# Two interleaved transformer layers on one core: an unsplit copy of half 0's last bank, interleaved scores in half 1, memory scores between weightings, and up weights loaded in the value part

## The chip, the cores and the metric

The kernel runs on one core of a Trainium2 chip. The metric is device time in microseconds; three executions of the kernel before took 1604.5, 1606.29 and 1607.28 us, so the median is 1606.29 us.

Five engines matter: TensorE (PE in the profile, and PEld for its weight loads, which overlap the matmuls), VectorE (DVE), ScalarE (ACT), GpSimd (POOL) and SyncE (SP), which issues most of the DMAs. TensorE writes its results into PSUM, which the kernel uses as eight banks; ACT and DVE copy them out to on-chip memory.

## The reference, cut to what matters

```
x = x + A(layernorm(x));  x = x + B(layernorm(x))     # done twice, with the same weights

A: for each of 64 segments of 32 tokens:
     h = concat(mem, segment)                # 8 memory rows + 32 token rows = 40 rows of 448
     q, k, v = h Wq, h Wk, h Wv              # 16 heads of 256
     p = softmax(mask(q k^T / 16))
     o = (p v) Wo
     mem = o[first 8 rows]                   # goes into the next segment
     output rows = o[other 32 rows]
B: (relu(x W_gate) * (x W_up)) W_down        # 448 -> 1792 -> 448
```

The memory makes attention a chain over segments: segment s+1 can't start before segment s has given its memory.

## The kernel before, in words

**Folded weights.** Per head, Wq and Wk are multiplied once into a 448x448 matrix (`A_sb`), and Wv and Wo into another (`B_sb`). This is the setup, in the pool `pre`: a loop over eight pairs of heads builds `A_sb` (the query-key part, lines 358-393) and a second one builds `B_sb` (the value part, lines 395-418). The raw weights are turned over by `flips` (line 307) into tiles with the tag `tT`, six buffers. The Wo blocks come by `load_wo` (line 349) over POOL's queue into four buffers with the tag `wo`; four are asked for in the last four passes of the query-key part, and each pass p of the value part asks for block p+4 at its end. `spread` (line 87) makes such a DMA wait for the TensorE instruction that was last in the program.

**Steps.** After the setup, 69 calls of `step` (line 680) follow. Step g works on segment g of the first layer pass ("chain 0") and on segment g-4 of the second ("chain 1"), so their 2 x 40 = 80 rows are the columns of one matmul. Steps 0 to 3 and 64 to 67 have one chain only, 40 columns. Heads are split in two halves (hf = 0, 1) of eight.

In a step, `project` (line 594) multiplies the rows with `A_sb`. A half is 28 tiles of 128, in five PSUM banks: tiles 0-5, 6-11, 12-17, 18-23 and 24-27; the copies go to `TQ` (the four banks of six tiles) and `TZ` (the bank of four). `BANKS` (line 42) sets the order; bank 18 comes last in both halves. `project_early` (line 581) does the 64-row part of four banks ahead. Then come the scores: `scores_m(hf)` (line 710) for the memory rows, into a bank `Sm`, and `scores_x(hf)` (line 718) for the token rows, into a bank `Sx`. Each score sums over four blocks kd of the 448 features in the order `KD = (0, 1, 3, 2)`: kd 0 and 1 read banks 0, 6 and 12, kd 3 reads `TZ`, and kd 2 reads banks 12 and 18. `softmax` (line 642) gives three pieces of work that the step places itself: maximum and difference on DVE, the exponential on ACT, the sum and the division on DVE. `flipped` turns the probabilities over on TensorE (tile `pps`, copied to `PT`), `weigh_m` (line 730) and `weigh_x` (line 743) multiply them with the rows (`ya`, `yb`; `y1`, `y2`) and copy the result to `Y`, and `project_out` and `project_last` multiply `Y` with `B_sb` into `ox` and `o`. The weighting of half 1's token rows is put off into the next step, as `late` (line 848), between `project_early(1, ...)` and half 1's projection.

**The feed-forward layer.** Every second step of the middle carries a `Feed` (here "a feed step"; the others are "plain steps"): 128 rows are normalised (`xn`), turned over (`tps`, `xT`), multiplied with W_up and W_gate (`ups`, `gps`), gated (`hh`, on DVE) and multiplied with W_down (`dps`). `open_rows` (line 488) takes four banks at a time and does the 64-row part first. W_up, W_gate and W_down are loaded in 28 pieces, one per call of `next_piece` (line 455), from step 0 on: 7 for W_up, 7 for W_gate, 14 for W_down.

**What sets the order.** All matmuls are chained in the order of the program (`in_order`, line 79), and after the setup DVE's and ACT's instructions are too (`InOrder`, line 92). A PSUM bank is chosen by `bank` (line 120): of the banks not held, the one that an own clock in the program says comes free first. A new tile in a bank waits for the last reader of the old one.

**The split copy.** In feed steps, half 0's bank 18 leaves PSUM in two copies on ACT (`quick`, lines 600, 620 and 631): tiles 0-2 after their nine matmuls, tiles 3-5 after the bank's last. Both halves lie in the same bank, and the matmuls of tiles 3-5 come behind the first copy.

Of the kernel before, what the change touches and what calls it, by code (L numbers as in the profile page):

```python
# [8 lines left out]
BF = mybir.dt.bfloat16  # L9
F32 = mybir.dt.float32  # L10
# [5 lines left out]
DM = 448  # L16
H = 16
NP = 8
# [3 lines left out]
L = MEM + SEG  # L22
F = 1792
# [36 lines left out]
def build_kernel(ctx, tc, A_x, A_mem0, A_Wq, A_Wk, A_Wv, A_Wo, B_W_gate, B_W_up, B_W_down, out,  # L60
# [149 lines left out]
    A_sb = glob.tile([P, 4, 2, NT, 128], BF, name="A_sb")  # L210
    B_sb = glob.tile([P, 2, NT, DM], BF, name="B_sb")

    hTb = []
    for i in range(2):
        t = glob.tile([P, BLK, HW], BF, name=f"hT{i}")
# [57 lines left out]
    with tc.tile_pool(name="pre", bufs=6) as pre:  # L273
# [32 lines left out]

        def flips(src, p, name):
            nat = load_nat(src, p, nc.sync)
            o = pre.tile([P, 4, 512], BF, tag="tT", name=name)

            def half(e2):
                tp = bank([P, 2, 512], BF, "tpw")
                n = 3 if src is Wv else 4
                for kd in range(n):
                    for e in range(2):
                        tr(tp[:, e, kd * 128:(kd + 1) * 128],
                           nat[:, kd, (2 * e2 + e) * 128:(2 * e2 + e + 1) * 128], ident[:])
# [29 lines left out]
        wos = []  # L347

        def load_wo(p):
            wos.append(pre.tile([P, 4, DM], BF, tag="wo", name="wo", bufs=4))  # L350
            spread(nc.gpsimd.dma_start(wos[-1][:], Wo[:, 4 * p:4 * p + 4, :]))

        ready, todo = queue(0)
# [4 lines left out]
        for p in range(NP):  # L358
# [26 lines left out]
                        todo.pop(0)()  # L385
            share(A_sb[:, 0:3, hf, 24 + p4, :], mx_ps[:, 0:3, :], 384, (1.28, 0.85))
            share(A_sb[0:64, 3, hf, 24 + p4, :], mx_ps[0:64, 3, :], 128, (1.28, 0.85))
            if p >= 4:
                load_wo(p - 4)
            if p == 1:  # L390
                xn0 = normed(row_stats(xp[1]))
            if p == 2:
# [2 lines left out]
        for p in range(NP):  # L395
            hf, p4 = divmod(p, 4)
            vT = ready
            ready, todo = flips(Wv, p + 1, "vT") if p + 1 < NP else (None, [])
            wo = wos.pop(0)
            for eo in range(2):  # L400
                for kd in range(3):
                    bps = bank([P, 512], F32, "bps")
                    for t in range(2):
                        e = 2 * eo + t
                        mm(bps[:, 0:DM], vT[:, e, kd * 128:(kd + 1) * 128], wo[:, e, :],
                           start=(t == 0), stop=(t == 1))
                    share(B_sb[:, hf, tidx(kd, eo, p4), 0:DM], bps[:, 0:DM], DM, (1.28, 0.85))
                    if kd == 1 and todo:
                        todo.pop(0)()
            bps = bank([P, 512], F32, "bps")  # L410
            for t in range(2):
                for eo in range(2):
                    e = 2 * eo + t
                    mm(bps[64 * eo:64 * eo + 64, 0:DM], v3[:, p, e, :], wo[:, e, :],
                       start=(t == 0), stop=(t == 1), tile_position=(0, 64 * eo))
            share(B_sb[:, hf, 24 + p4, 0:DM], bps[:, 0:DM], DM, (1.28, 0.85))
            if p + 4 < NP:
                load_wo(p + 4)

    for i in range(min(3, nblk)):  # L420
        nc.gpsimd.memset(xa[i][:], 0.0)
# [19 lines left out]
    nc.gpsimd.memset(hh[:], 0.0)  # L441

    Wg_sb = main.tile([P, 4, F], BF, name="Wg_sb")
    Wu_sb = main.tile([P, 4, F], BF, name="Wu_sb")
    Wd_sb = main.tile([P, FT, DM], BF, name="Wd_sb")
    pieces = []
    for dst, src in ((Wu_sb, B_W_up), (Wg_sb, B_W_gate)):
        for k in range(3):
            for cols in (slice(0, F // 2), slice(F // 2, F)):
                pieces.append((dst[:, k, cols], src[128 * k:128 * k + 128, cols]))  # L450
        pieces.append((dst[FR[src is B_W_gate], 3, :], src[384:448]))
    for f in range(FT):
        pieces.append((Wd_sb[:, f, :], B_W_down[128 * f:128 * f + 128]))

    def next_piece():

        if pieces:
            spread(nc.sync.dma_start(*pieces.pop(0)))


    class Feed:

# [131 lines left out]
    def project(hf, chains, hb, j, banks, pre={}, busy=False, first=None, inside=None):  # L594

        n = L * len(chains)
        for i0, k in banks:
            ps = pre[i0] if i0 in pre else bank([P, 512], F32, "prj")
            two = len(chains) == 2
            quick = busy and not hf and i0 == 18  # L600

            def copies(eng, rows, T, a, b):
                T = T.rearrange("p g (t q) -> p t g q", q=16)
                if two:
                    evac(eng, T, ps[rows, a * n:b * n].rearrange("p (t g q) -> p t g q", t=b - a, q=16))
                    return
                c = chains[0]
                src = ps[rows, a * n:b * n].rearrange("p (t w) -> p t w", t=b - a)
# [5 lines left out]
            def tq(a, b):  # L614
                return TQ[hf][:].rearrange("p g u w -> p g (u w)")[:, :, 16 * (i0 + a):16 * (i0 + b)]
# [12 lines left out]
            if first is not None:  # L628
                first()
            if i0 < 24:  # L630
                a = 3 if quick else 0
                copies(act if (i0 != 6 if busy and hf else i0 % 12) else dve, slice(0, P), tq(a, k), a, k)
            else:
                copies(act if busy else dve, slice(0, 64), TZ[hf][0:64, :, 0:64], 0, k)
                copies(act, slice(64, 128), TZ[hf][64:128, :, 64:128], 0, k)
            if i0 in (6, 18):
                next_piece()

# [41 lines left out]
    def step(g, ff, pre, late):  # L680
# [26 lines left out]
            act.copy(hk[:, 4, 64:128], kps[:, 3, 64:128])  # L707
            return hk

        def scores_m(hf):  # L710
            if not ms:
                return (lambda: None,) * 3
            Sp = bank([P, 2, L], F32, "Sm", 1100)
            for kd in KD:
                mm(Sp[:, :, :], queries(hf, 2, kd), moving(hb, j, kd, (0, 1)), start=(kd == KD[0]), stop=(kd == KD[-1]))
            return softmax(Sp, 2, PM[hf], blk[:], f"m{hf}")

        def scores_x(hf):
            Sp = bank([P, 4, L], F32, "Sx", 2500 if hf == 0 else 3500 if ff is None else 8000)
            both = len(chains) == 2  # L720
            if not both:
                mm(Sp[:, :, :], ident[:], maskS[:], start=True, stop=False, skip_group_check=True)
            for half in range(2):
                for c in chains:
                    for kd in KD:
                        mm(Sp[:, 2 * half + c, :], queries(hf, 3 * c + half, kd), moving(hb, j, kd, (c,)),
                           start=(both and kd == KD[0]), stop=(kd == KD[-1]), skip_group_check=True)
            return softmax(Sp, 4, PX[hf], None, f"x{hf}", maskS[:] if len(chains) == 2 else None)

        def weigh_m(hf, hk, PT):  # L730
            if not ms:
# [11 lines left out]
        def weigh_x(hf, hk, PT):  # L743

            def keep(eng, c, t0, src):
                n = src.shape[-1] // SEG
# [98 lines left out]
        if ff is not None:  # L845
            ff.norm()
        pre1 = project_early(1, chains, hb, j)
        if late is not None:
            late()
        if len(chains) == 1:  # L850
            m0 = scores_m(0)
            m0[0]()
            m0[1]()
        project(1, chains, hb, j, BANKS[1][0:1], pre1, True)
        if len(chains) == 2:
            m0 = scores_m(0)
            m0[0]()
            m0[1]()
# [11 lines left out]
        project(1, chains, hb, j, BANKS[1][4:5], pre1, True, None, flip_m0)  # L870
        if ff is not None:
            ff.xposed_out()
        x0 = scores_x(0)
        weigh_m(0, hk, pm)
        m1 = scores_m(1)
        m1[0]()
        m1[1]()
        x1 = scores_x(1)
        x0[0]()
        if end:  # L880
            ff.open_rows((0, 1))
# [42 lines left out]
        else:  # L924
# [118 lines left out]
```

## Time and profile before

| what | value |
|---|---|
| median of three runs | 1606.29 us |
| the profiled execution | 1606.33 us |
| its span, first to last instruction | 1604.4 us |
| PE busy / PEld busy | 1573.1 us (98%) / 1445.3 us (90%) |
| DVE / ACT / POOL busy | 1133.0 (71%) / 757.4 (47%) / 77.4 us (5%) |
| granted TensorE clock | 1.00 |
| DMA, mean over the span | 21 GB/s; 200 to 330 GB/s in the first 50 us |
| share of PE in the chain that ended last | 96% |

The profiled execution lies 0.04 us from the median, and 1.9 us of it are outside the span. Two things are needed to read the profile. A matmul's end is modelled: an 80-column matmul is shown with 202 ns, though the next one starts some 36 ns after it. So a stall is seen better between the starts of two matmuls than in idle time, which is smaller by the part of the 202 ns that lies over it. And a group of matmuls in the timeline ends about 0.2 us after the start of its last one.

By time, the span has: the query-key part until about 48 us, the value part until about 75 us, one-chain steps with the loads of the feed-forward weights until about 145 us, pairs of a plain and a feed step with two chains from there to about 1516 us (30 such feed steps, one every 45.9 us), and the one-chain steps and the last feed at the end.

### The profile page before, as it was taken

The page shows a single profiled execution, that of the slowest core. Times are in us where ns is not written, and L with a number is a line of the kernel's source. Part 1 is how long each engine was busy: PE and PEld are TensorE (multiplying, and loading weights), DVE is VectorE, ACT ScalarE, POOL GpSimd, SP SyncE. Part 2 cuts the span into 40 slices and gives each one's busy share as a digit, 9 for nine tenths or more (in the row PEclk, how much of TensorE's full clock was granted, in tenths as well). Part 3 has the DMA queues.
Part 4 walks back from the last instruction along what each step waited for, and adds up shares of the span by engine and source line. Part 5 has one row for each costly group of instructions (what it writes and reads, how often), then busy time and mean ns, then how long its engine had stood idle before and what let it go on. Part 6 is the DMA issues. An engine that isn't in the chain of part 4 may idle for free.

```text
span 1604.4 us, 89783 instructions
## 1 busy us (share of the span) xinstructions
PE 1573.1 (98%) x41132; PEld 1445.3 (90%) x41132; DVE 1133.0 (71%) x3706; ACT 757.4 (47%) x2126; POOL 77.4 (5%) x172
## 2 busy tenths in 40 slices
PE   9999999999999999999999999999999999999998
PEld 6688999999999999999999999999999999999897
DVE  8766777777677777776777777767777777667765
ACT  5644444454444444544444445444444454444443
POOL 3200000000000000000000000000000000000000
PEclk9999999999999999999999999999999999999999
DMA  8530000000000000000000000000000000000000
GB/s 242 163 107 15 8 9 9 10 4 9 9 10 9 9 9 9 4 9 10 9 9 9 9 8 5 10 9 9 9 9 9 7 5 10 9 8 6 7 7 6
DMA packets 27755, 33.12 MB, mean 21 GB/s; under 512 B 3560, under 2 KB 26480, under 8 KB 27376
## 3 DMA queue, kind: packets, MB, share of 16 engines
q1 hardware_dynamic: 26288, 23.70, 5.3%
q8 instruction: 321, 5.26, 1.3%
q0 software_dynamic: 1088, 3.68, 0.8%
q14 instruction: 58, 0.48, 0.1%
HBM read 23.70 MB, written 1.84 MB: 16 GB/s over the span
## 4 chain that ended last, share of the span: by engine, by line
PE 96%; ACT 1%; DVE 1%; issue 1%; DMA 0%; SPq 0%; POOLq 0%; ACTq 0%; POOL 0%
PE prj L143 31%; PE ox L143 25%; PE ups L143 7%; PE dps L143 5%; PE gps L143 5%; PE o L143 5%; PE y L143 4%; PE Sx L143 3%; PE pps L151 2%; PE Sm L143 2%; PE bps L143 1%; PE aps L143 1%; PE tpw L151 1%; PE ya L143 1%; PE tps L151 1%; PE yb L143 1%
## 5 line engine op out<-in xcount | busy, mean ns | idle before, releaser
L143 PE MATMUL prj<-hT,A_sb 128*128 128x80 bf16 (+3 forms) x15232 | 547.1, 199 | 17.3 <-ACT TQ L101 16.6
L143 PEld LDWEIGHTS <-A_sb 128*128 128x128 bf16 (+1 forms) x15232 | 500.8, 99 | 42.9 <-issue 21.2
L143 PEld LDWEIGHTS <-B_sb 128*128 128x128 bf16 (+1 forms) x15232 | 490.6, 103 | 14.5 <-issue 1.0
L143 PE MATMUL ox<-Y,B_sb 128*128 128x80 bf16 (+3 forms) x11424 | 440.3, 199 | 0.9 <-issue 0.9
L101 ACT CAST TQ<-prj 128x480 bf16<-128x480 f32 (+5 forms) x416 | 189.6, 466 | 111.4 <-PE prj L143 101.4
L101 DVE CAST Y<-y 128x256 bf16<-128x256 f32 x376 | 151.4, 457 | 55.5 <-PE y L143 55.4
L101 ACT CAST Y<-y 128x512 bf16<-128x512 f32 (+2 forms) x392 | 136.6, 419 | 103.4 <-PE y L143 103.2
L101 ACT ACTIVATE se<-se 128x80 f32<-128x80 f32 (+1 forms) x270 | 81.9, 303 | 165.5 <-DVE se L101 161.2
L143 PE MATMUL gps<-xT,Wg_sb 128*128 128x128 bf16 (+3 forms) x1904 | 133.9, 216 | 0.0
L101 DVE CAST TQ<-prj 128x480 bf16<-128x480 f32 (+1 forms) x228 | 128.4, 572 | 7.5 <-PE prj L143 7.0
L143 PE MATMUL ups<-xT,Wu_sb 128*128 128x128 bf16 (+3 forms) x1904 | 132.3, 216 | 0.5 <-DVE xT L101 0.5
L101 DVE SCALAR_TENSOR_TENSOR hh<-gps,ut 128x512 bf16<-128x512 f32 (+2 forms) x136 | 80.2, 592 | 47.6 <-PE ya L143 41.4
L143 PEld LDWEIGHTS <-Wu_sb 128*128 128x128 bf16 (+1 forms) x1904 | 105.0, 97 | 8.0
L143 PEld LDWEIGHTS <-hk 40*128 40x128 bf16 (+1 forms) x1950 | 99.4, 96 | 10.7 <-issue 2.5
L143 PEld LDWEIGHTS <-Wg_sb 128*128 128x128 bf16 (+1 forms) x1904 | 106.9, 97 | 0.5 <-issue 0.5
L101 ACT CAST TZ<-prj 64x320 bf16<-64x320 f32 (+2 forms) x264 | 96.8, 377 | 17.2 <-DVE TZ L101 13.6
L101 ACT COPY os<-o 64x16 f32<-64x16 f32 (+3 forms) x135 | 25.8, 191 | 162.2 <-PE o L143 160.6
L101 DVE TENSOR_REDUCE ssum<-se 128x2 f32<-128x80 f32 (+1 forms) x270 | 73.7, 273 | 37.5 <-ACT se L101 37.5
L143 PE MATMUL dps<-Wd_sb,hh 128*128 128x448 bf16 (+1 forms) x476 | 93.1, 353 | 0.0
L143 PEld LDWEIGHTS <-TQ 128*128 128x128 bf16 x1938 | 87.1, 97 | 6.0 <-issue 0.4
L143 PE MATMUL y<-PT,hk 40*128 40x256 bf16 (+1 forms) x1280 | 86.7, 248 | 1.6 <-ACT PT L101 1.0
L235 POOL TENSOR_SCALAR rstd<-mv 128x1 f32<-128x1 f32 x67 | 14.8, 221 | 1467.2 <-DVE mv L101 1467.2
(118 smaller groups left out, 1920.0 us busy)
## 6 DMA issues: line engine op xcount, KB each, us to landing
wo<-in_A_Wo_dram POOLq DMA_DIRECT2D x8, 448.0 KB, 4.6
nat<-in_A_Wq_dram SPq DMA_DIRECT2D x8, 384.0 KB, 4.9
nat<-in_A_Wk_dram SPq DMA_DIRECT2D x8, 384.0 KB, 5.0
nat<-in_A_Wv_dram SPq DMA_DIRECT2D x8, 384.0 KB, 5.7
xa<-in_A_x_dram SPq DMA_DIRECT2D x32, 56.0 KB, 2.2
xa<-xp SPq DMA_DIRECT2D x32, 56.0 KB, 1.9
out_dram<-xa SPq DMA_DIRECT2D x32, 56.0 KB, 2.3
xp<-in_A_x_dram SPq DMA_DIRECT2D x30, 56.0 KB, 2.6
```

The costliest lines, as they stand in the source:

```text
L101: r = f(*a, **k)
L143: in_order(nc.tensor.matmul(out, lhsT, rhs, **k))
L151: in_order(nc.tensor.transpose(out, src, idn))
L235: nc.gpsimd.tensor_scalar(out=rstd[:], in0=mv[:, 1:2], scalar1=EPS, scalar2=None, op0=ALU.add)
```

## The change

Five edits:

1. `quick` is gone: bank 18 of half 0 leaves in one copy after its last matmul, in feed steps too.
2. `scores_m` and `scores_x` become one function `scores(hf, m, x)`. For half 1 it does the memory and the token scores together: first all matmuls of the blocks kd 0, 1 and 3 of both, then those of kd 2. Half 0 keeps its order.
3. W_up's tile is taken at the start of the kernel, outside the pools, and its seven pieces are asked for in the value part, two at the end of each pass from p = 3 on. To make room, `tT` has four buffers instead of six and `wo` three instead of four; Wo's first three blocks are asked for in the last three passes of the query-key part, and pass p of the value part asks for block p+3. The calls of `next_piece` in the steps stay, and begin with W_gate.
4. In one-chain steps half 0's memory scores, with the first two pieces of their softmax, move from behind the late weighting into it, between the copies of `y1` and the matmuls of `y2`.
5. In plain one-chain steps the turn of half 1's memory probabilities comes after 23 instead of 22 tiles of `project_out`.

```diff
+    Wu_sb = glob.tile([P, 4, F], BF, name="Wu_sb")
...
+    pieces = weights(Wu_sb, B_W_up)
...
-            o = pre.tile([P, 4, 512], BF, tag="tT", name=name)
+            o = pre.tile([P, 4, 512], BF, tag="tT", name=name, bufs=4)
...
-            wos.append(pre.tile([P, 4, DM], BF, tag="wo", name="wo", bufs=4))
+            wos.append(pre.tile([P, 4, DM], BF, tag="wo", name="wo", bufs=3))
...
-            if p >= 4:
-                load_wo(p - 4)
+            if p >= 5:
+                load_wo(p - 5)
...
-            if p + 4 < NP:
-                load_wo(p + 4)
+            if p + 3 < NP:
+                load_wo(p + 3)
+            if p >= 3:
+                next_piece()
+                next_piece()
...
+    pieces += weights(Wg_sb, B_W_gate)
...
-            quick = busy and not hf and i0 == 18
...
-                if quick and i == 3:
-                    copies(act, slice(0, P), tq(0, 3), 0, 3)
...
-        def scores_m(hf):
-        def scores_x(hf):
+        def scores(hf, m, x):
...
+            def mem(kds):
+                for kd in kds:
+                    mm(Sm[:, :, :], queries(hf, 2, kd), moving(hb, j, kd, (0, 1)),
+                       start=(kd == KD[0]), stop=(kd == KD[-1]), skip_group_check=True)
+
+            def own(kds):
+                for half, c in groups:
+                    for kd in kds:
+                        mm(Sx[:, 2 * half + c, :], queries(hf, 3 * c + half, kd), moving(hb, j, kd, (c,)),
+                           start=(both and kd == KD[0] and (half, c) == groups[0]), stop=(kd == KD[-1]),
+                           skip_group_check=True)
...
+            if m and x:
+                mem(KD[:3])
+                mask()
+                own(KD[:3])
+                mem(KD[3:])
+                own(KD[3:])
...
             for c in chains:
                 keep(act if c == 0 or len(chains) == 1 else dve, c, 0, y1[c][:])
+            if between is not None:
+                between()
             y2 = {c: bank([P, 384], F32, f"y2_{c}", 1300) for c in chains}
...
-            late()
-        if len(chains) == 1:
-            m0 = scores_m(0)
+            late(memory_0 if len(chains) == 1 else None)
+        if len(chains) == 1 and late is None:
+            memory_0()
...
-        x0 = scores_x(0)
+        _, x0 = scores(0, False, True)
         weigh_m(0, hk, pm)
-        m1 = scores_m(1)
+        m1, x1 = scores(1, True, True)
         m1[0]()
         m1[1]()
-        x1 = scores_x(1)
         x0[0]()
...
-            late_flip = 23 if hi - lo == W else 22
+            late_flip = 23
...
-        return pre, lambda: weigh_x(1, hk, px1)
+        return pre, lambda between: weigh_x(1, hk, px1, between)
```

`memory_0` is `scores(0, True, False)` and the first two pieces of its softmax; in two-chain steps it is called where `scores_m(0)` was.

More of the change, by code (lines that the diff above doesn't have):

```diff
@@ L211, in build_kernel, with weights, next_piece @@
     B_sb = glob.tile([P, 2, NT, DM], BF, name="B_sb")
+    Wu_sb = glob.tile([P, 4, F], BF, name="Wu_sb")
+    def weights(dst, src):
+        return [(dst[:, k, cols], src[128 * k:128 * k + 128, cols])
+                for k in range(3) for cols in (slice(0, F // 2), slice(F // 2, F))] + [
+                    (dst[FR[src is B_W_gate], 3, :], src[384:448])]
+    pieces = weights(Wu_sb, B_W_up)
+    def next_piece():
+        if pieces:
+            spread(nc.sync.dma_start(*pieces.pop(0)))
     hTb = []
@@ L443, in build_kernel @@
     Wg_sb = main.tile([P, 4, F], BF, name="Wg_sb")
-    Wu_sb = main.tile([P, 4, F], BF, name="Wu_sb")
+    pieces += weights(Wg_sb, B_W_gate)
     Wd_sb = main.tile([P, FT, DM], BF, name="Wd_sb")
[L446 to L451, printed above, removed]
     for f in range(FT):
         pieces.append((Wd_sb[:, f, :], B_W_down[128 * f:128 * f + 128]))
-    def next_piece():
-        if pieces:
-            spread(nc.sync.dma_start(*pieces.pop(0)))
     class Feed:
@@ L599, in project, with copies @@
             two = len(chains) == 2
-            quick = busy and not hf and i0 == 18
-            def copies(eng, rows, T, a, b):
+            def copies(eng, rows, T):
                 T = T.rearrange("p g (t q) -> p t g q", q=16)
                 if two:
-                    evac(eng, T, ps[rows, a * n:b * n].rearrange("p (t g q) -> p t g q", t=b - a, q=16))
+                    evac(eng, T, ps[rows, 0:k * n].rearrange("p (t g q) -> p t g q", t=k, q=16))
                     return
                 c = chains[0]
-                src = ps[rows, a * n:b * n].rearrange("p (t w) -> p t w", t=b - a)
+                src = ps[rows, 0:k * n].rearrange("p (t w) -> p t w", t=k)
                 x, m = (0, SEG) if c == 0 else (MEM, 0)
@@ L612, in copies @@
                      src[:, :, x:x + SEG].rearrange("p t (g q) -> p t g q", q=16))
-            def tq(a, b):
-                return TQ[hf][:].rearrange("p g u w -> p g (u w)")[:, :, 16 * (i0 + a):16 * (i0 + b)]
             for i in range(k):
@@ L630, in project @@
             if i0 < 24:
-                a = 3 if quick else 0
-                copies(act if (i0 != 6 if busy and hf else i0 % 12) else dve, slice(0, P), tq(a, k), a, k)
-            else:
-                copies(act if busy else dve, slice(0, 64), TZ[hf][0:64, :, 0:64], 0, k)
-                copies(act, slice(64, 128), TZ[hf][64:128, :, 64:128], 0, k)
+                T = TQ[hf][:].rearrange("p g u w -> p g (u w)")[:, :, 16 * i0:16 * (i0 + k)]
+                copies(act if (i0 != 6 if busy and hf else i0 % 12) else dve, slice(0, P), T)
+            else:
+                copies(act if busy else dve, slice(0, 64), TZ[hf][0:64, :, 0:64])
+                copies(act, slice(64, 128), TZ[hf][64:128, :, 64:128])
             if i0 in (6, 18):
@@ L708, in hk_make, with mask @@
             return hk
-        def scores_m(hf):
+        def scores(hf, m, x):
             if not ms:
[L712 to L716, printed above, removed]
-        def scores_x(hf):
-            Sp = bank([P, 4, L], F32, "Sx", 2500 if hf == 0 else 3500 if ff is None else 8000)
-            both = len(chains) == 2
[L721 to L728, printed above, removed]
+                m = False
+            both = len(chains) == 2
+            Sm = bank([P, 2, L], F32, "Sm", 1100) if m else None
+            Sx = bank([P, 4, L], F32, "Sx", 2500 if hf == 0 else 3500 if ff is None else 8000) if x else None
+            groups = [(half, c) for half in range(2) for c in chains]
+            def mem(kds):
[8 more added lines that the diff above has]
+                           skip_group_check=True)
+            def mask():
+                if not both:
+                    mm(Sx[:, :, :], ident[:], maskS[:], start=True, stop=False, skip_group_check=True)
+            if m and x:
[4 more added lines that the diff above has]
+                own(KD[3:])
+            elif m:
+                mem(KD)
+            elif x:
+                mask()
+                own(KD)
+            sm = softmax(Sm, 2, PM[hf], blk[:], f"m{hf}") if m else (lambda: None,) * 3
+            sx = softmax(Sx, 4, PX[hf], None, f"x{hf}", maskS[:] if both else None) if x else None
+            return sm, sx
@@ L741, in weigh_m, with weigh_x @@
             act.copy(YB[hf][:, 16:28, M0:M0 + 16], yb[:].rearrange("p (t q) -> p t q", q=16))
-        def weigh_x(hf, hk, PT):
+        def weigh_x(hf, hk, PT, between=None):
             def keep(eng, c, t0, src):
@@ L847, in step, with memory_0 @@
         pre1 = project_early(1, chains, hb, j)
-        if late is not None:
-            late()
-        if len(chains) == 1:
-            m0 = scores_m(0)
+        m0 = None
+        def memory_0():
+            nonlocal m0
+            m0, _ = scores(0, True, False)
             m0[0]()
             m0[1]()
+        if late is not None:
+            late(memory_0 if len(chains) == 1 else None)
+        if len(chains) == 1 and late is None:
+            memory_0()
         project(1, chains, hb, j, BANKS[1][0:1], pre1, True)
         if len(chains) == 2:
-            m0 = scores_m(0)
-            m0[0]()
-            m0[1]()
+            memory_0()
         project(1, chains, hb, j, BANKS[1][1:2], pre1, True, m0[2])
```

## The prediction

> **What bounds the kernel now.** I read the page's busy shares first, then who waited for whom, then the timeline of one feed step, matmul by matmul.
>
> ```profile
> PE 1573.1 (98%) x41132; PEld 1445.3 (90%) x41132; DVE 1133.0 (71%) x3706; ACT 757.4 (47%) x2126; POOL 77.4 (5%) x172
> ```
>
> TensorE is the bound: the chain that ended last is 96% PE. No edit takes a matmul away or makes one shorter, so only stalls of TensorE can go. The largest wait of PE:
>
> ```profile
> PE prj L143 <- ACT TQ L101: 16.6, 33, 0.5
> ```
>
> 33 times 0.5 us is one per feed step. In the timeline of the feed step near 299 us:
>
> ```profile
> 297.31 1.53 PE L143 MATMUL prj<-hT,A_sb 128*128 128x80 bf16 x38
> 298.93 0.36 ACT L101 CAST TQ<-prj 128x240 bf16<-128x240 f32 x1
> 299.34 1.02 PE L143 MATMUL prj<-hT,A_sb 128*128 128x80 bf16 x33 [0.50 <-ACT TQ L101]
> 299.86 0.36 ACT L101 CAST TQ<-prj 128x240 bf16<-128x240 f32 x1 [0.57 <-PE prj L143]
> 300.20 0.61 PE L143 MATMUL y<-PT,hk 40*128 40x256 bf16 x10
> 300.65 1.22 DVE L101 CAST Y<-y 128x512 bf16<-128x512 f32 x3 [0.44 <-PE y L143]
> ```
>
> The reader is to see the split copy's first part (128x240) end at 298.93 + 0.36 = 299.29 and the next matmul start 0.05 us later. The group before ends at 298.84, so its last matmul started at 298.64 (0.20 earlier, the modelled length). Matmuls of 80 columns follow one another by 0.036 us (18 of them take 0.82 us: (0.82 - 0.20)/17). So the stall is 299.34 - 298.64 - 0.036 = **0.66 us**, more than the 0.50 shown as idle. The wait is for the program's own read of the bank that TensorE writes next.
>
> A second stall hides in the scores of half 1, in every two-chain step:
>
> ```profile
> 304.58 0.56 ACT L101 CAST TQ<-prj 128x480 bf16<-128x480 f32 x1 [0.36 <-PE prj L143]
> 304.95 0.24 PE L143 MATMUL Sm<-hT,TQ 128*128 128x80 bf16 x2
> 305.02 0.20 PE L143 MATMUL Sm<-hT,TZ 128*128 128x80 bf16 x1
> 305.19 0.21 PE L143 MATMUL Sm<-hT,TQ 128*128 128x80 bf16 x1
> ```
>
> The fourth matmul of `Sm` (kd 2) should start 0.036 after 305.02; it starts at 305.19, 0.05 after the copy's end at 305.14. Stall: 0.14 us. In the plain step at 286 us the same pair is at 285.93 and 286.05: 0.08 us. The list of waits has neither, since the modelled ends cover them.
>
> A third kind lies in the one-chain steps:
>
> ```profile
> 85.93 0.23 PE L143 MATMUL yb<-PT,hk 128*128 128x64 bf16 x2 [0.50 <-issue]
> 89.94 0.34 PE L143 MATMUL ox<-Y,B_sb 128*128 128x40 bf16 x7 [0.86 <-issue]
> 93.94 0.84 PE L143 MATMUL prj<-hT,A_sb 128*128 128x40 bf16 x35 [0.23 <-issue]
> 98.04 0.30 PE L143 MATMUL prj<-hT,A_sb 128*128 128x40 bf16 x6 [0.42 <-issue]
> 105.77 0.27 PE L151 MATMUL pps<-ident,PX 128*128 128x128 bf16 x2 [0.56 <-issue]
> ```
>
> Nothing that the profile shows is awaited there. They add up to 2.6 us idle, with 0.16 us more each under the modelled ends: 3.4 us. Four are 4.0 to 4.1 us apart. The instruction queue moves 5.26 MB in 321 packets, 16 KB each; 256 instructions of an estimated 64 bytes (5.26 MB over 82,264 PE and PEld rows) are 4.2 us at the 61 rows per us of 80 to 90 us. So I read them as instruction blocks that come late while weight pieces load (0.50 of the DMA engines from 80 to 100 us). In the one-chain steps after 1516 us, without loads, there are none.
>
> **The change part by part.**
>
> *The unsplit copy.* It takes 0.66 us out of each of 33 feed steps: 21.8 us. What is late next? The one copy takes 0.56 (128x480, mean 558 ns) and starts 0.24 after the bank's last matmul, as the second part did. With TensorE 0.66 earlier, that is 299.20 to 299.76, and 299.81 with the 0.05 to TensorE. ACT's next work, `y1`, begins at 300.67 - 0.66 = 300.01, so nothing on ACT is pushed. Half 0's `Sm` reads `TQ` at 301.39 - 0.66 = 300.73: 0.9 us of cover. But following `bank` through a pair of steps by hand, chain 1's `y2` takes the bank of half 0's tiles 18-23. It starts 0.22 after the first `y` (two pairs of 0.11), at 300.42 - 0.66 = 299.76, and has to wait until 299.81: 0.05 back. On DVE the two `xn` pieces are bound to POOL (299.57) and end at 300.21 whatever TensorE does; the copy of chain 1's `y1`, due at 299.99, then starts at some 300.13 and ends at 300.82, and half 1's TZ bank, which takes that PSUM bank at 301.53 - 0.66 = 300.87, gets it at 300.88: 0.01. One-chain feed steps have no chain-1 `y`. Sum: 30 x (0.66 - 0.06) + 3 x 0.66 = **-20 us**.
>
> *Interleaved scores, feed steps.* 12 `Sx` matmuls of 0.025 us (0.10 per four) come ahead of kd 2, which is due at 305.02 + 0.036 + 0.30 = 305.36, after the copy. The 0.14 goes. But `Sm` now ends at 305.56 instead of 305.39; DVE's `mx` starts at 305.59 instead of 305.44, and from there to the gating `hh` at 308.43 DVE is never idle, so `hh` of tile group 0 ends at 309.12 + 0.15 = 309.27. Its `gps` bank is the one that `open_rows((2, 3))` takes for group 3, due at 309.36 - 0.15 = 309.21: it waits until 309.32. Gain 0.15, loss 0.11: 30 x 0.04 = **-1 us**. Bounds: 30 x 0.15 gained (no wait) to nothing.
>
> *Interleaved scores, plain steps.* 0.08 goes. `Sm` ends 0.21 later for DVE, whose chain to `PM` ended at 288.34 + 0.24 = 288.58; its turn on TensorE loads weights at 288.93. After: 288.79 + 0.05 against 288.85, just in time. 31 x 0.08 = **-2.5 us**; bounds 0 to -2.5.
>
> *Up weights.* The pieces go behind Wv's loads on SP in the built order, and run in the value part beside Wo, where the DMA engines are 0.34 to 0.58 busy. TensorE's use of them is at 129 us, so the earlier landing itself is worth nothing. Wo's loads take 4.0 to 4.6 us in the value part; a pass is 3.55 us (POOL's issues at 51.91, 55.46, 59.01). With three buffers block p+3 is asked for 6.7 us ahead of use: 2 us to spare. The first three, at 39.9, 44.7 and 48.5, land after 7.4, 6.0 and 4.6 us, at 47.3, 50.7 and 53.1, for passes at 48.0, 51.5 and 55.1. POOL's five memsets (5.2 us) slide by one pass behind the last Wo issue, to about 72 us; `hk` is first needed after 76. Four `tT` buffers hold what one pass reads and the next fills. So 0 in the setup. From 77 us on, 21 pieces are loaded instead of 28: W_gate where W_up was, the half-sized W_down pieces where W_gate was. Under W_up two blocks were due and one was late, under W_gate all three, under W_down one of five or six. I expect two late blocks instead of five: **-1.7 us**; bounds 0 and -3.4.
>
> [...]
>
> *One-chain steps.* Seven have a late weighting with memory scores moved into it. Going from the 40-row `y` to 128-row matmuls costs 0.12 us (`y` to the next `Sm` at 110.26 and 110.41, less 0.03); now it happens twice, and coming back costs 0.015: 7 x 0.13 = 0.9. The copy of bank 18 ends at 110.14, near where `Sm` will be (110.2), so little wait is added. Against it, at 1521.6 `Sm` waited 0.4 for a `y` copy, and that bank changes. The interleaving delays `Sm` by some 0.2 where DVE's chain is already late for TensorE (the plain one-chain turns; `PX` at 131.72; both turns near 172), 8 places; `late_flip` gives 0.075 back in five. Sum: 0.9 - 0.4 + 8 x 0.2 - 0.4 = **+1.7 us**; bounds 0 and +3.
>
> *Sum:* -20 - 1 - 2.5 - 1.7 + 1.7 = -23.5 on the profiled execution's 1606.33 us (span 1604.4), which lies 0.04 from the median: **1582.8 us**, span 1580.9.
>
> **The rivals.**
>
> *The bubble is refilled (chance 0.17).* TensorE runs 0.6 us earlier against POOL's `xn` and DVE. For it: two of the waits that I found have 0.05 us or less of play. If another 0.3 us per pair comes back, 30 x 0.3 = 9: 1592. Against it: DVE idles 1.36 us ahead of `hh` and 0.7 ahead of `xp` in each feed step.
>
> *No new wait (0.12).* All stalls go and none returns: 33 x 0.66 + 30 x 0.15 + 2.5 + 3.4 = 32: 1574.
>
> *Fetch is hidden (0.08).* By the mechanism in which the five waits don't depend on loads, they stay, and the sum is 1.7 higher: 1584.5. [...]
>
> *The stall is not the split copy's (0.03).* If the wait on ACT was only the last of several and another reader holds the bank, the 20 us stay: 1603. Against it: the copy's end and the matmul's start are 0.05 apart.
>
> *Slower (0.02).* The Wo loads starve: W_up's pieces lengthen them beyond the 6.7 us that three buffers leave, and each late pass is paid in full by TensorE. Blocks 3 to 7 would have to land after 6.7 + 25/5 = 11.7 us on average to end above 1606; the longest landing in the trace is 7.4 us, at full DMA load.
>
> **How the numbers follow.** My forecast, 1582.8, has 0.58. Its own terms run from 1578 to 1587. The range reaches from the no-new-wait case, with a little left of it outside, to the refilled one: 1575 to 1592. About 0.2% (3.2 us) is what a measurement here can tell from no change; faster by more has 0.95 (all but the last two rivals), within 0.2% has 0.03, slower 0.02.
>
> **What would show it.** Right: PE's wait on `TQ` (16.6 us, 33) is gone; a copy of 128x480 where the two of 128x240 were; no gap inside `Sm`; in feed steps `gps` of group 3 starting some 0.05 after `hh` ends; fewer waits on "issue" before 110 us; a pair of steps 45.9 - 0.72 = 45.2 us long. Wrong: a new wait of `y`, `prj` or `ups` in every pair, `bps` waiting for `wo`, or a span between 200 and 1500 us that shrinks by less than 28 x 0.6.

## The result, and the profile after

The changed kernel takes 1586.06 us (median of 4 runs, 1585.16 to 1587.05) against 1606.47 us for the kernel before on the same chip: ratio 0.9875, 95% interval 0.9858 to 0.9892, so 20.4 us less. The forecast was 23.5 us less, 1582.8 us. The profiled execution took 1585.9 us with a span of 1583.8 us; the span shrank by 20.6 us.

The busy shares of the kernel after. No matmul was taken away, and PE is at 99%:

```profile
PE 1570.4 (99%) x41132; PEld 1444.0 (91%) x41132; DVE 1130.9 (71%) x3706; ACT 753.1 (48%) x2090; POOL 77.4 (5%) x172
```

The longest waits of PE after (total, times, longest, in us). The wait for `TQ`, 16.6 us in 33 pieces before, is not in the list any more, and nothing of its kind has come in its place:

```profile
PE junk L143 <- DVE still L170: 1.2, 1, 1.2
PE y L143 <- ACT PT L101: 1.0, 2, 0.5
PE pps L151 <- DVE PM L101: 1.0, 2, 0.5
PE y L143 <- ACT Y L101: 0.8, 2, 0.6
```

The timeline of the feed step that was shown of before, now some 4 us earlier:

```profile
295.74 0.56 ACT L101 CAST TQ<-prj 128x480 bf16<-128x480 f32 x1 [0.45 <-PE prj L143]
...
296.02 0.71 PE L143 MATMUL y<-PT,hk 40*128 40x256 bf16 x10
...
296.50 0.59 ACT L101 CAST Y<-y 128x512 bf16<-128x512 f32 x1 [0.20 <-PE y L143]
296.61 0.68 DVE L101 CAST Y<-y 128x512 bf16<-128x512 f32 x1
```

One copy of 128x480 stands where two of 128x240 were, and no `prj` row waits. But the ten `y` matmuls now take 0.71 us, where before it was 0.61. In the trace the first `y2` starts alone at 296.247, and its partner of the other chain, which takes the copied bank, at 296.353: 0.05 after the copy ended (295.74 + 0.56 = 296.30). Before, the two started together.

The scores of half 1 in the same step:

```profile
300.50 0.56 ACT L101 CAST TQ<-prj 128x480 bf16<-128x480 f32 x1 [0.36 <-PE prj L143]
...
300.88 0.24 PE L143 MATMUL Sm<-hT,TQ 128*128 128x80 bf16 x2
300.94 0.20 PE L143 MATMUL Sm<-hT,TZ 128*128 128x80 bf16 x1
...
301.29 0.20 PE L143 MATMUL Sm<-hT,TQ 128*128 128x80 bf16 x1
```

The last `Sm` matmul, kd 2, comes at 301.29, 0.23 after its copy ended at 301.06, with twelve `Sx` matmuls ahead of it. The stall is gone. What was to be late next is late:

```profile
304.51 1.28 DVE L101 SCALAR_TENSOR_TENSOR hh<-gps,ut 128x512 bf16<-128x512 f32 x2
...
305.14 0.22 PE L143 MATMUL ups<-xT,Wu_sb 64*128 64x128 bf16 x1
305.25 0.21 PE L143 MATMUL gps<-xT,Wg_sb 64*128 64x128 bf16 x1
```

Before, these two started together:

```profile
309.36 0.22 PE L143 MATMUL ups<-xT,Wu_sb 64*128 64x128 bf16 x1
309.36 0.22 PE L143 MATMUL gps<-xT,Wg_sb 64*128 64x128 bf16 x1
```

In the other groups of the step `ups` and `gps` of the two row halves still do; here `gps` of tile group 3 comes 0.11 later. The first of the two `hh` ended at 305.198, `gps` began at 305.252.

A pair of steps takes 45.26 us, before 45.92 (mean of 28 pairs, by the first `kps` of a step): 0.66 us less, forecast 0.72.

Matmul by matmul, start to start, the 20.6 us of span divide so: 29 two-chain feed steps -17.0, 28 plain steps -2.0, the one-chain steps and their neighbours -1.35, the setup -0.2. In the -1.35 there is a loss that nobody forecast. In the last attention step the 84 `ox` matmuls of 64 columns took 2.62 us before:

```profile
1583.73 2.62 PE L143 MATMUL ox<-Y,B_sb 128*128 128x64 bf16 x84
```

and after

```profile
1561.58 4.17 PE L143 MATMUL ox<-Y,B_sb 128*128 128x64 bf16 x84
```

The table of stretches says why (PE, PEld, DVE, ACT, POOL busy, then the granted clock, the DMA share and GB/s):

```profile
1558.00:1560.00 2.00, 1.49 (x41) 1.31 (x38) 1.46 (x7) 1.09 (x4) 0.00 (x0) 1.00 0.03 8
1560.00:1562.00 2.00, 1.49 (x22) 1.13 (x21) 1.21 (x4) 1.54 (x5) 0.00 (x0) 0.95 0.00 0
1562.00:1564.00 2.00, 2.00 (x42) 2.00 (x40) 0.00 (x0) 0.49 (x3) 0.00 (x0) 0.50 0.04 8
1564.00:1566.00 2.00, 2.00 (x60) 1.95 (x59) 0.00 (x0) 0.00 (x0) 0.00 (x0) 0.70 0.00 0
```

The granted clock was 0.5 for 3.41 us, from 1561.81, and from one of these matmuls to the next it was 53 to 54 ns instead of 29 to 30: 1.55 us lost.

### The profile page after: what moved, and what is told of

The parts are those of the page before. It is cut to its first block, busy times and chain, and to the rows that moved or that the text cites. A ratio compares the mean times of both kernels' runs of the same rounds, so it can differ in the third digit from the quotient of the medians.

```text
span 1583.8 us, 89753 instructions
## 1 busy us (share of the span) xinstructions
PE 1570.4 (99%) x41132; PEld 1444.0 (91%) x41132; DVE 1130.9 (71%) x3706; ACT 753.1 (48%) x2090; POOL 77.4 (5%) x172
## 3 DMA queue, kind: packets, MB, share of 16 engines
q8 instruction: 321, 5.26, 1.4%
## 4 chain that ended last, share of the span: by engine, by line
PE 97%; DVE 1%; ACT 0%; DMA 0%; issue 0%; SPq 0%; POOLq 0%; POOL 0%; ACTq 0%
PE prj L143 31%; PE ox L143 25%; PE ups L143 7%; PE dps L143 5%; PE gps L143 5%; PE o L143 5%; PE y L143 4%; PE Sx L143 3%; PE pps L151 2%; PE bps L143 1%; PE aps L143 1%; PE Sm L143 1%; PE tpw L151 1%; PE ya L143 1%; PE kps L151 1%; PE tps L151 1%
## 5 line engine op out<-in xcount | busy, mean ns | idle before, releaser
L143 PE MATMUL prj<-hT,A_sb 128*128 128x80 bf16 (+3 forms) x15232 | 541.6, 199 | 0.1
L101 ACT CAST TQ<-prj 128x480 bf16<-128x480 f32 (+1 forms) x380 | 184.2, 497 | 102.9 <-PE prj L143 96.2
L143 PE MATMUL gps<-xT,Wg_sb 128*128 128x128 bf16 (+3 forms) x1904 | 137.2, 215 | 0.0
L101 ACT COPY os<-o 64x16 f32<-64x16 f32 (+3 forms) x135 | 25.7, 191 | 163.2 <-PE o L143 161.6
L143 PE MATMUL y<-PT,hk 40*128 40x256 bf16 (+1 forms) x1280 | 91.2, 248 | 1.9 <-ACT PT L101 1.0
L101 ACT COPY PT<-pps 128x256 bf16<-128x256 bf16 (+1 forms) x136 | 47.2, 347 | 81.1 <-PE pps L151 76.9
```

Source lines behind the costliest of these rows:

```text
L101: r = f(*a, **k)
L143: in_order(nc.tensor.matmul(out, lhsT, rhs, **k))
```

## The experiments

The kernel before was timed again beside the experiments and had medians of 1607.14 (beside the first four kernels), 1605.51 (the next four) and 1608.37 us (the last four), so ratios to it are compared.

**One copy, alone.** The kernel before with

```
-            quick = busy and not hf and i0 == 18
+            quick = False
```

> The kernel before with edit 1 alone: bank 18 of half 0 leaves in one copy. Theory (the gap was the split copy's own wait, and 0.1 us per two-chain feed step comes back where the y2 matmuls of chain 1 wait for the whole copy): each of 30 two-chain feed steps loses 0.66 - 0.11 = 0.55 us and each of 3 one-chain ones 0.67, 18.5 us in all, so some 1588 us; PE's wait for TQ (16.6 us, 33 times) is gone. Rival (the other edits carry the gain, the gap only moves to another reader of the bank): 1600 us or more.

1589.15 us, ratio 0.9891 (0.9876 to 0.9906), 18.0 us less. In the two-chain feed steps the gap between the `prj` matmuls shrinks by 0.661 us, as forecast, and the `y` matmuls grow by 0.114 on average, where 0.06 was forecast for everything that comes back. In 29 of the 30 steps it is 0.10; in one, near 1202 us, it is 0.38, because there the copy on ACT began 0.28 us later than in the others, for a reason that the trace doesn't name. The copy causes both; the other edits have no part in them.

**Interleaved scores, alone.** The kernel before with the new `scores`, its calls where `scores_m` and `scores_x` stood, and nothing else.

> The kernel before with edit 2 alone: half 1's memory and token scores interleaved. Theory (the 0.14 us inside Sm goes in feed steps, but 0.11 comes back where gps of group 3 waits for hh; in plain steps 0.07 goes for good): 30 x 0.03 + 31 x 0.07 = 3.1 us less, less about 1 us in one-chain steps whose softmax chain is late: 1604 us. Rival (the wait goes and nothing comes back): 30 x 0.14 + 31 x 0.08 = 6.7 us less, 1599.6 us.

1604.38 us, ratio 0.9984 (0.9975 to 0.9993), 2.8 us less. A feed step gains 0.138 inside the scores and loses 0.112 at `gps`; a plain step gains 0.073. So the loss at `hh` belongs to the interleaving.

**Up weights late again.** The changed kernel with W_up in `pieces` where W_gate is, four `wo` and the old number of `tT` buffers:

```
-            if p >= 3:
-                next_piece()
-                next_piece()
...
-    pieces += weights(Wg_sb, B_W_gate)
+    pieces += weights(Wu_sb, B_W_up) + weights(Wg_sb, B_W_gate)
```

> The changed kernel with edit 3 undone: W_up is loaded from step 0 on, Wo has four buffers, tT six. Theory (TensorE's instruction blocks come late while weight pieces load in one-chain steps): the waits on issue return, about five between 80 and 110 us with some 2.6 us idle, and the time is 3 us longer, 1589 us. Rival (block fetches are hidden and these waits have nothing to do with the loads): no such waits and 1586 us.

1587.00 us, ratio 0.988 (0.9865 to 0.9895): not to be told from the changed kernel's 0.9875. In the trace the issue waits are back, 3.2 us of them in four places. But see below: this one trace says less than it seems.

**Memory scores behind the weighting again.** The changed kernel with `late(None)` and, in all one-chain steps, `memory_0()` behind it.

> The changed kernel with edit 4 undone: in one-chain steps half 0's memory scores come behind the late weighting again. Theory (going between 40-row and 128-row matmuls twice costs 0.24 us in each of six steps, and the earlier softmax is worth nothing): 1.4 us less, 1584.6 us. Rival (the earlier softmax spares TensorE a wait for PM or for a y bank, 0.6 us at the first one-chain step after the middle): no gain, 1586 us or more.

1585.91 us, ratio 0.9871 (0.9855 to 0.9888): no difference in time. In the trace, against the changed kernel's, each of six steps gains 0.24 us where the memory scores no longer break into the weighting (`y` to `Sm` -0.05, `Sm` to `y` -0.13, `y` to `prj` -0.15, between `y` +0.10), and `PM`'s turns, later again, take back 0.75 in all, which leaves 0.66. It was covered by issue waits that this execution had more of. It had them at the end too, where the DMA engines were almost idle (0.03 busy from 1550 to 1560 us in the changed kernel's trace):

```profile
1551.52 0.32 PE L143 MATMUL prj<-hT,A_sb 64*128 64x40 bf16 x12 [0.72 <-issue]
```

**kd 2 after the first half of the Sx groups.**

```
-                own(KD[:3])
-                mem(KD[3:])
-                own(KD[3:])
+                k = len(groups) // 2
+                own(KD[:3], groups[:k])
+                mem(KD[3:])
+                own(KD[:3], groups[k:])
+                own(KD[3:])
```

> The changed kernel with the last block of half 1's memory scores behind six of the token matmuls instead of twelve. Theory (DVE's chain of two softmaxes, 0.15 us late, makes gps of group 3 wait 0.11 us for hh in each two-chain feed step; the copy of bank 18 ends 0.17 after the third Sm matmul, and six matmuls of 0.025 just cover it): the gap inside open_rows goes, 30 x 0.11 = 3.3 us less, and up to 0.5 us less in one-chain steps: 1582.3 us. Rival (the 0.11 is not hh's, or the wait for TQ returns): no change, 1586 us.

1581.42 us, ratio 0.9851 (0.9837 to 0.9866). Six `Sx` matmuls still cover the copy, `Sm` ends earlier, and `gps` of group 3 no longer waits:

```profile
303.17 1.34 DVE L101 SCALAR_TENSOR_TENSOR hh<-gps,ut 128x512 bf16<-128x512 f32 x2
...
303.94 0.22 PE L143 MATMUL gps<-xT,Wg_sb 64*128 64x128 bf16 x1
303.99 0.22 PE L143 MATMUL gps<-xT,Wg_sb 64*128 64x128 bf16 x1
```

The rows are 0.05 apart, as in the other groups. A feed step is 0.110 us shorter, the gap at `gps` 0.112: the wait for `hh` was the whole loss. The one-chain turns give back 0.7 us more in all.

**The banks of y2 exchanged.** `for c in reversed(chains)` where the two `y2` banks are taken, so that chain 0 has the copied bank.

> The changed kernel with the two y2 banks of a two-chain step exchanged, so that chain 0's y2, which goes first, takes the bank of half 0's tiles 18-23. Theory (the copy of these tiles ends 0.05 us after y2 is due, and the loss is 0.1 because chain 0's matmul starts alone and its pair with chain 1's is broken): the pair starts together 0.05 late, 30 x 0.05 = 1.5 us less, 1584.5 us. Rival (the loss is the wait itself, whoever has it): no change.

1586.99 us, ratio 0.9886 (0.9871 to 0.99): nothing gained. The trace has the same 0.11 us ahead of `y2`, now in front of both chains (297.476 to 297.689), plus 0.02 in feed and plain steps alike. The theory that the wait is dear because it breaks the pair falls. The wait is simply 0.10 long: the copy ends 0.05 later than was forecast.

**Work in the last two waits.** The changed kernel with two matmuls on a tile of zeros ahead of each of the last two weightings; they are extra work.

> The changed kernel with two 512-column matmuls of zeros, read by nobody, in each of the two waits for PT in the last attention step. Theory (the two idle stretches of 0.5 us lower the activity that the chip measures, the clock falls to half for 3.4 us, and 64 output matmuls take 1.5 us longer): granted clock 1.00 from 1550 us to the end of the matmuls, and 1.5 us less than the profiled execution of the changed kernel. Rival (the fall has another cause, such as the length of the run): the clock falls as before and the time is the same or longer.

1584.43 us, ratio 0.9869 (0.9855 to 0.9884). The clock did not fall (mean 1.000, against 0.998 in the changed kernel's profiled execution). But of nine kernels without this work (the kernel before, the changed one, the six experiments above and the next one below) only the changed one has a fall in its trace, so the run decides nothing. That the chip measures an activity is the theory's assumption; no run shows it. The one with longer waits, below, says more.

**Loads beside one-chain steps at the end.** The changed kernel with 16 pieces of W_gate loaded once more into a spare tile from step 64 on; extra work.

> The changed kernel with 16 loads of 224 KB into a spare tile that nobody reads, one per call of next_piece from step 64 on, when only one chain is left. It adds loads that the reference does not need. Theory (in one-chain steps TensorE uses up instruction blocks so fast that a load beside the fetch makes a block late): waits on issue appear there, some 4 us apart, 0.2 to 0.9 us each, 1 to 3 us in all; none of them is in the changed kernel at that place. Rival (no tie to the loads): none appear and the time is unchanged.

1584.64 us, ratio 0.9873 (0.9857 to 0.989). The loads ran, at a DMA share of 0.22 to 0.49 (0.18 to 0.76 between 80 and 100 us in the kernel before), and PE stayed busy:

```profile
1505.00:1510.00 5.00, 5.00 (x165) 4.90 (x162) 3.50 (x16) 1.64 (x6) 0.00 (x0) 1.00 0.49 160
1510.00:1515.00 5.00, 5.00 (x156) 4.79 (x154) 2.76 (x14) 1.95 (x6) 0.00 (x0) 1.00 0.22 58
1515.00:1520.00 5.00, 5.00 (x178) 4.57 (x175) 3.75 (x17) 3.70 (x20) 0.79 (x2) 1.00 0.44 141
```

Not one issue wait came. With the theory of loads as the cause in doubt, two kernels left the loads out.

**No weight loads, kernel before; and up loads only, changed kernel.** In the first

```
-            spread(nc.sync.dma_start(*pieces.pop(0)))
+            dst, _ = pieces.pop(0)
+            spread(nc.gpsimd.memset(dst, 0.0))
```

and in the second the same for the pieces of W_gate and W_down alone.

> The kernel before, with all 28 pieces of W_up, W_gate and W_down written as zeros by POOL at the same points instead of loaded; it leaves out these loads, so the feed-forward part computes with zeros. Theory (instruction blocks come late because weight loads run beside them): no wait on 'issue' on TensorE between 76 and 125 us, where the four kernels that load all 28 pieces there had 1.0 to 3.2 us of idle time in such waits; about 1603.5 us against 1606. Rival (the blocks are late by themselves in these steps, loads or not): 1 to 3 us of waits stay, at matmuls that lie a multiple of 128 apart, and the time stays within 1 us of 1606.

1605.75 us, ratio 0.9982 (0.9974 to 0.9991), 2.6 us less. Two rows still wait, with no feed-forward weight loaded:

```profile
88.85 0.34 PE L143 MATMUL ox<-Y,B_sb 128*128 128x40 bf16 x7 [0.39 <-issue]
```

and one at 103.86 us with 0.28.

> The changed kernel with W_up loaded as there, and the 21 pieces of W_gate and W_down written as zeros by POOL instead of loaded; it leaves out these loads. Six kernels that load 21 pieces there had 0 to 1.6 us of issue waits between 76 and 125 us, 0.94 on average. Theory (loads make the blocks late): 0, and 1585 us against the changed kernel's 1586. Rival (late by themselves): about 1 us of waits stays, 1586.

1584.73 us, ratio 0.9854 (0.9841 to 0.9867), and no issue wait before 125 us. Neither theory has both results.

What the waits have in common came out when the matmuls of the traces were counted. Before 126 us every such gap lies at matmul 976, 1104, 1232, 1360, 1487, 1615, 1743, 1871, 1999, 2255 or 2382 of its trace: 128 apart or a multiple of it, if a missing record or two are allowed for. At the end the kernel with edit 4 undone has them at 39870, 39998, 40254 and 40382. With its weight loads, 128 matmuls are 256 rows, the block that the prediction estimated from 5.26 MB in 321 packets. So the waits are read as late instruction blocks, as forecast, at fixed points of the stream. The packets of the instruction queue in the traces bear this out: every one of the 38 waits on issue between 75 and 126 us in the fourteen traces, and the four gaps at the end just named, came to an end 1.24 to 1.72 us after such a packet had landed, while the middle four fifths of all matmuls of that stretch lie anywhere from 0.4 to 3.9 us behind the last landing. The packets themselves took 0.96 to 1.21 us there on average, 1.06 with 28 pieces loaded in the kernel before and 1.14 with none: no longer beside loads. How late a block is differs from execution to execution. The sum of the gaps (over the usual start-to-start time) at these points, to 126 us:

| pieces loaded from 77 us | gaps, us, one execution of each kernel | mean |
|---|---|---|
| 28 | 3.4 (before), 2.2, 2.0, 4.5 | 3.0 |
| 21 | 0.9 (after), 2.4, 0.7, 2.0, 1.8, 1.9, 2.9, 3.6 | 2.0 |
| none | 1.9, 0 | 1.0 |

The means go the way of the forecast, but the single values overlap, and the group without loads has two.

**Longer waits at the end.** The changed kernel with `PT` copied twice more on ACT before each of the last two weightings.

> The changed kernel with two more copies of each PT in the last attention step, so that the two waits of TensorE of 0.51 us near 1560 us become some 1.3 us each; the added copies are work that the computation does not need. In the changed kernel's trace the granted clock was 0.5 from 1561.8 to 1565.2 us; in nine other traces with the same two waits it was not. Theory (enough idle time in the stretch before makes the clock fall): it falls again for 3.4 us and the 84 ox matmuls take 4.2 us instead of 2.6; span about 1582.2 + 1.6 + 1.55 = 1585.4. Rival (the fall came by chance, whatever the idle time): no fall, span 1583.8.

Span 1590.0 us, from one execution. The waits became 1.39 and 1.33 us, and the clock fell for 6.83 us, twice 3.41:

```profile
1562.00:1564.00 2.00, 0.61 (x16) 0.51 (x13) 0.74 (x4) 1.40 (x5) 0.00 (x0) 1.00 0.00 0
1564.00:1566.00 2.00, 0.70 (x7) 0.43 (x6) 1.28 (x4) 1.92 (x6) 0.00 (x0) 0.89 0.00 0
1566.00:1568.00 2.00, 1.96 (x25) 1.57 (x25) 0.00 (x0) 1.03 (x3) 0.00 (x0) 0.50 0.00 0
1568.00:1570.00 2.00, 2.00 (x42) 2.00 (x40) 0.00 (x0) 0.00 (x0) 0.00 (x0) 0.50 0.03 8
```

So with longer waits the fall came back; which quantity decides is taken up at the end. The span is 4.6 above the expected 1585.4. Against the changed kernel's trace the issue waits of steps 0 to 3 and 66 were 3.2 us longer; the second stretch at half clock explains more of it.

**The best of both.** The changed kernel with kd 2 after half the groups and the memory scores behind the weighting.

> The changed kernel with kd 2 of the memory scores after the first half of the Sx groups, and the one-chain memory scores back behind the late weighting. The first alone gave 1581.4. By the trace of the kernel with edit 4 undone, the move between the weightings costs 0.24 us in each of 6 steps and gives 0.75 back at the turns of PM: 0.66 net. Theory: 1580.8 us. Rival (edit 4 pays after all): 1582.

1582.70 us, ratio 0.9843 (0.9829 to 0.9856), 25.7 us below its kernel before. The kernel with kd 2 after half the groups alone had 0.9851 (0.9837 to 0.9866): the 0.66 us are in this trace too (each of steps 1 to 3, 65 and 66 has the four changes of `y`, `Sm` and `prj`), but the times can't tell the two apart.

## Why the prediction was right, and where it was short

| term | forecast | measured in the trace |
|---|---|---|
| one copy | -20 | 30 x (0.661 - 0.114) + 3 x 0.67 = -18.4 |
| scores, feed steps | -1 | 30 x (0.138 - 0.112) = -0.8 |
| scores, plain steps | -2.5 | 28 x 0.073 = -2.0 |
| up weights | -1.7 | -2.5 in this trace; about -1 by the means |
| one-chain steps | +1.7 | about +2.2 (not measured by itself: what the other terms leave of the -1.35) |
| clock in the last attention step | none | +1.55 |
| setup and the rest | 0 | -0.6 |

The right-hand column adds up to -20.6. The bounds that the prediction gives for its single terms, added up, reach from 1576 to 1589 us, somewhat wider than the "1578 to 1587" that it states.

*What bounds.* Right: only stalls of TensorE went, and the stall of 0.66 us, longer than the 0.50 idle that the profile shows, came back as 0.661.

*The unsplit copy.* The mechanism held to the last step: `y2` of chain 1 has to wait for the copy. The mis-sized term is "0.05 back": it was 0.114. The step that failed is the time of the copy, "that is 299.20 to 299.76": moved by the 3.51 us by which this place is earlier, it ran from 299.25 to 299.81. It took the forecast 0.56; it began late. The prediction let it begin "0.24 after the bank's last matmul, as the second part did", and it began 0.29 after. The trace of before had both lags: the split copy's first part began at 298.93, 0.29 after the matmul at 298.64. Of ACT's copies from `prj` to `TQ` there, between 150 and 1500 us, the 176 that wait for TensorE alone begin 0.24 after their last matmul, and 148 of the 150 that also wait on a second semaphore begin 0.29 after it. The unsplit copy is of the second kind. Half of the 3.1 us by which the profiled execution missed the forecast is here (30 x 0.054 = 1.6). The 0.01 us at the TZ bank can't be seen.

*Interleaved scores.* Right in both signs, 0.15 gained and 0.11 lost forecast, 0.138 and 0.112 measured. The experiment that keeps six `Sx` matmuls ahead shows that the loss could be avoided: the cover needed was 0.14 us, and twelve matmuls are twice that.

*Up weights.* In the pair of traces the waits fell, as forecast, and they are late blocks, shown by their places and by the landings of the packets. "Instruction blocks that come late while weight pieces load" was at most part of the cause: gaps occur without any load (1.9 us in the kernel before without loads, 0.72 us in one row at 1551 us), and 16 loads at the end made none. Counting late blocks under each kind of piece had no basis. The 2.5 us of the one pair of traces are partly luck: 0.9 us in the changed kernel is the second lowest of eight. What makes a block late, and why the first one-chain steps have more of it than the last, stays open. On the rival of a hidden fetch: between 125 and 1400 us neither the kernel before nor the changed one has a wait on issue, while up to seven blocks in the first steps of 40-column matmuls came late, by 0.1 to 1.3 us each. The rival's price for this change, waits that stay as they were, is not ruled out: the means fell by 1.0 us, but the single values overlap.

*One-chain steps.* The two parts were +0.5 for the move (0.9 less 0.4 for the `y` copy) and +1.2 for later turns. The move cost 0.66 by the undone edit. That the later turns took the rest was not measured by itself; PE's waits for `PM`, 0.3 us in one place before and 1.0 us in two after, point that way. The 0.13 for a transition was about half of what a break costs (0.24), and the gain at `PM`'s turns made up for most of it.

*The rivals.* No refilled bubble beyond the named waits: the only new ones are 0.114 and 0.112 on average in each feed step. `bps` gained no wait for `wo`.

*What was missed.* The clock. Two waits of 0.51 us were in the trace of before, without a fall. Whether they cost 1.55 us more went with how they lay in time, as the last section shows; the prediction had no term for that. Of the executions that were only timed the record has the mean granted clock alone. A mean of 0.998 is at least 4.8 us at half clock, of which the end of the span, behind the last matmul, gives at most 1.9 in the traces, so such an execution had a fall: one of the three of the changed kernel (1587.05 us, its slowest) and 5 of 35 of the kernel before, beside the experiments. So the kernel before has falls too, in some of its executions.

## What to carry to other kernels

When a stall is removed, follow the freed bank or buffer to its next user and take the lag of the step that releases it from a copy in the trace that waits for the same things: here the next wait was named rightly and was twice its size, which is 1.6 us over thirty steps. When work is pushed ahead of a late operand, push no more than the wait is long, since whoever reads the delayed result pays for the surplus (here `gps`, 0.112 us in each feed step). And a term of 2 us that varies by 1 us between executions can't be settled by one pair of traces: several kernels that leave the stretch as it is serve as repeats.

## What the runs showed of the hardware

*The granted clock fell on a grid.* In the changed kernel's trace the clock was full for 1556.48 us, then 0.5 for 3.41, then full for 17.07, which is five times 3.4133; the first stretch is 456 times that. In the trace of the kernel before it was full for 1597.44 us, 468 times that. Cut into stretches of this length, the one before the fall holds both waits on `PT`, 1.03 us without a matmul. Of the twelve traces with the same two waits, three have both in one stretch, and two of these fell (the changed kernel and the one with up loads only; the one with kd 2 after half the groups did not). In the nine where the grid splits them, with up to 0.93 us idle in one stretch there, none fell. With 2.23 us it fell for two stretches. The idle time alone does not decide, though: in the trace with interleaved scores alone, a stretch at 101.20 us has 1.19 us without a matmul and no fall behind it, and in the one with longer waits the clock stayed at 0.5 behind a stretch with 0.49.

Another count separates them. Add up the columns of all matmuls that start in a stretch, each weighted by its rows out of 128; a `y` matmul, 40 rows by 256 columns, counts 80. Apart from stretches at the end without any matmul, the clock was 0.5 behind the stretches with 896, 2688, 2688 and 2752 such columns, and full behind all others of the fourteen traces, nearly 6,500 in number, the lowest of which have 3136, 3232 (the one of three that did not fall) and 3272 (the one with 1.19 us idle). A stretch in the middle of the span has some 7200. So what went with a fall, in these traces, was how little matmul work a stretch held: 2752 columns or fewer with it, 3136 or more without. In the changed kernel's trace the two waits beside the 40-row `y` matmuls left 2688. The count was found after the fact, and no run was built to test it.

*Instruction blocks came late at fixed matmuls.* In the one-chain steps, and most of all in the first ones, TensorE waited 0.1 to 1.3 us at some of the matmuls that lie 128 apart; the 38 waits there that the profile puts down to issue ended 1.24 to 1.72 us after an instruction packet had landed.
